# Joined maxima over both halves of the keys in the first unit of an attention kernel, with a second set of key differences

## The chip, the cores and the metric

The kernel runs on one core of one Trainium2 chip, as one launch. The metric is the device time of the launch in microseconds (us), lower being better. A core has five engines that work side by side and wait for each other on semaphores: TensorE (matrix products, shown as PE, its weight loads as PEld), VectorE (DVE), ScalarE (ACT), GpSimd (POOL) and SyncE (SP), which here only issues transfers. Transfers between the chip's main memory and the core's own memory (SBUF) run on 16 DMA engines. Products of TensorE land in PSUM, eight banks of 128 x 512 numbers of 4 bytes, from which VectorE and ScalarE read them.

## The reference

Two independent computations whose results stand side by side in the output. The first (A) is a long convolution over 2048 positions and 448 channels, whose filter is a sum of 256 complex exponentials per channel. The second (B) is full attention with 16 heads of 28 channels:

```python
def _B_ref(x, wqkv, wo):
    B, S, D = x.shape                      # 1, 2048, 448
    H = 16; Dh = D // H
    qkv = (x @ wqkv).reshape(B, S, 3, H, Dh).transpose(2, 0, 3, 1, 4)
    q, k, v = qkv[0], qkv[1], qkv[2]
    scores = jnp.einsum("bhqd,bhkd->bhqk", q, k) * Dh ** -0.5
    p = _softmax(scores, axis=-1)
    o = jnp.einsum("bhqk,bhkd->bhqd", p, v)
    return o.transpose(0, 2, 1, 3).reshape(B, S, D) @ wo
```

All data are 32-bit floats. The softmax needs the largest score of each query before it takes exponentials; the change is about how these maxima are found for one part of the queries.

## The kernel before

**Stages.** The first 204 us hold the *projections* (x times wqkv, as products of split numbers, a high and a low part) and, woven between them, the *seeds* of the convolution's exponentials, computed in eight groups (`seeds(o)`, o = 0 to 7) on ScalarE, VectorE and GpSimd. Then come the maxima of the first unit, and then the *attention loop*, which also carries the rest of the convolution. A *unit* is one group of four heads (`g`, 0 to 3) with one chunk of 512 queries (`c`, 0 to 3); there are 16, and the first is group 0 with chunk 0.

**Projections.** `work` lists the jobs: for each chunk c of 512 positions, `qk_proj(c, s, g)` for four groups and for k (s = 1) and q (s = 0), and four `v_proj`. Each job is twelve matmuls into one of three PSUM tiles (`pm`) and an `evac` that splits the result into a high and a low part on ScalarE and VectorE (tile `hl`, two buffers) and stores it in main memory (`k_d`, `q_d`, `v_d`). For k of chunks 0 and 1 the evacuation also forms *key differences*: the first half of the chunk's keys minus the second half, again as high and low part (`kb`, `dhl`), stored in `kd_d`. The steps `t` of the seeds' pipeline (41 of them) set the pace; projections are spread over the first 37 (`PW`). `ahead` puts loads between the steps: from step `A0` on the first differences, from step `A1` on the first unit's queries. At step 37 the last projection has been issued, the memory of the projection weights (`wst`) is given back, and the pool of the first keys (`k0_p`) takes its place. Up to here a scheduler orders each engine's instructions; from the attention loop on they stand in the order in which the code issues them.

**Maxima.** For a block of 128 queries of one head (16 blocks, index `i`, four heads `j` times four blocks `t`) and 2048 keys, the scores of a block come in four products of 512 columns (`kc` = 0 to 3), each in its own PSUM bank. Because max(a, b) = b + relu(a - b), the first two products are joined: `kc` = 0 multiplies the queries with the key differences (tile `kdif`), and ScalarE takes the Relu into SBUF (tile `rl`, two buffers); `kc` = 1 multiplies them with the second halves of the same two chunks, and one VectorE instruction adds the two and takes the maximum (the custom operation `rl<-pm,rl`). So one pass over 512 columns covers 1024 keys. `kc` = 2 and 3 are plain products with a plain maximum each (`mx<-pm`). `max_join` takes the largest of the three numbers of a block, `max_end` turns them, and `max_put` writes them as two more rows into the query tile. For the first unit the PSUM tiles are taken in turn from a ring of five (`more`: two of `pt`, three of `pm`); in the attention loop the maxima of the next unit run between the other work, with three blocks of lead (`LEAD`).

**Loads.** Keys (`khat`, four tiles of one head each), queries (`qhat`, three buffers, used by the seeds too), differences (`kdif`, one tile a head) and v come back from main memory in rows of 32 partitions, four transfers for a tile. Heads 0 and 1 of the first keys are issued by ScalarE, all other transfers by Sync. Each engine issues in its own order, and a transfer waits for the one eight places before it in the program, so that at most eight are under way. The lines that order the stage:

```python
            if t + 1 == PW:
                project()
                wst.close()
                k0_p = pool(k0_st, "k0_p", side="right")
                for j in range(HG):
                    load_k(0, j, k0_p, nc.scalar if j < 2 else nc.sync)
                load_q(1)
                for c in range(NQ):
                    load_v(0, c)
```

All calls pass through one recording helper, so the profile shows nearly every instruction at line 75 (L75); what is meant is read from the tiles' names.

Of the kernel before, what the change touches and what calls it, by code (L numbers as in the profile page):

```python
# [40 lines left out]
PS = 1  # L41
SGB, XB, XL = 2, 5, 4
K0, KP, KD, UP = 0, 3.5, 5, 3
A0, A1 = 26, 34

N1 = 32
N2 = 64
# [43 lines left out]
def body(ctx, tc, a, out):  # L91
# [11 lines left out]
    dram = ctx.enter_context(tc.tile_pool(name="dram", bufs=1, space=DRAM))  # L103
    k_d = [dram.tile([2, 128, L], F32, name=f"k_{g}") for g in range(G)]
    kd_d = [dram.tile([2, 128, CQ], F32, name=f"kd_{g}") for g in range(G)]
    q_d = [[dram.tile([2, 128, CQ], F32, name=f"q_{g}_{c}") for c in range(NQ)] for g in range(G)]
    sd_d = [dram.tile([BO, 128, SDF], F32, name=f"sd_{o}") for o in range(NO)]
    yu_d = dram.tile([128, N1, D], F32, name="yu_d")
# [46 lines left out]
    def load_kd(g, j, rows=range(4)):  # L155
        if 0 in rows:
            kd_g[g, j] = kd_p.tile([128, CQ], F32R, name=f"kdif{j}")
        t = kd_g[g, j]
        for r in rows:
            nc.sync.dma_start(t[32 * r:32 * r + 32].bitcast(F32), kd_d[g][r % 2, 32 * j:32 * j + 32, :])  # L160

    def load_q(u, rows=range(4)):
        g, c = divmod(u, NQ)
# [3 lines left out]
        for r in rows:  # L167
            nc.sync.dma_start(t[32 * r:32 * r + 32].bitcast(F32), q_d[g][c][r // 2].rearrange("(j p) q -> p j q", j=HG))

    def max_mm(u, i, kc, ps=w_tile):  # L170

        if i == 0 and kc == 0:
            m_u[u] = q_p.tile([128, HG, 4, 3], F32, name="mx", bufs=2)
        j, t = divmod(i, 4)
        pm = ps()
        q, kt = q_u[u][:, j, t * 128:(t + 1) * 128], kt_g[u // NQ][j]
        mx = m_u[u][:, j, t, max(kc - 1, 0):max(kc - 1, 0) + 1]
        if kc == 0:
            nc.tensor.matmul(pm, q, kd_g[u // NQ, j], start=True, stop=True)
            rl_u[u, i] = kd_p.tile([128, CQ], F32, name="rl", bufs=2)  # L180
            nc.scalar.activation(rl_u[u, i], pm, AF.Relu)
        elif kc == 1:
            kb = kt.rearrange("p (c s n) -> p c s n", c=NQ, s=2)[:, :2, 1, :]
            nc.tensor.matmul(pm.rearrange("p (c n) -> p c n", c=2), q, kb, start=True, stop=True)
            rl = rl_u.pop((u, i))
            nc.vector.tensor_tensor_reduce(rl, pm, rl, 1.0, -3.0e38, ALU.add, ALU.max, mx)
        else:
            nc.tensor.matmul(pm, q, kt[:, kc * CQ:(kc + 1) * CQ], start=True, stop=True)
            nc.vector.tensor_reduce(mx, pm, axis=AX.X, op=ALU.max)

    def max_join(u):
        m_u[u, 1] = q_p.tile([128, HG * 4], F32, name="m1", bufs=2)
        nc.vector.tensor_reduce(m_u[u, 1], m_u[u].rearrange("p a b c -> p (a b) c"), axis=AX.X, op=ALU.max)

    def max_end(u, ps):
        nc.tensor.transpose(ps[:16, :128], m_u[u, 1], ident)
# [12 lines left out]
    with ExitStack() as st:  # L209
# [237 lines left out]
        def qk_proj(c, s, g):  # L447
# [9 lines left out]
            def evac():  # L457
                hl = x_p.tile([128, 2, CQ], F32R, name="hl", bufs=2)
                th, tl = hl[:, 0], hl[:, 1]
                if s == 1:  # L460
                    nc.scalar.activation(th, pp, AF.Identity, bias=kones)
                    nc.vector.scalar_tensor_tensor(tl, pp, kones, th.bitcast(F32), op0=ALU.add, op1=ALU.subtract)
                else:
                    nc.scalar.activation(th, pp, AF.Copy)
                    nc.vector.tensor_tensor(tl, pp, th.bitcast(F32), ALU.subtract)
                if s == 1 and c < 2:
                    HC = CQ // 2
                    kb = y_p.tile([128, HC], F32, name="kb")
                    dhl = y_p.tile([128, 2, HC], F32R, name="dhl")
                    dh, dl = dhl[:, 0], dhl[:, 1]  # L470
                    nc.scalar.activation(kb, pp[:, HC:], AF.Copy)
                    nc.vector.tensor_tensor(kb, pp[:, :HC], kb, ALU.subtract)
                    nc.scalar.activation(dh, kb, AF.Copy)
                    nc.gpsimd.tensor_tensor(dl, kb, dh.bitcast(F32), ALU.subtract)
                    nc.sync.dma_start(kd_d[g][:, :, c * HC:(c + 1) * HC].rearrange("i p l -> p i l"), dhl.bitcast(F32))
                nc.sync.dma_start((k_d[g][:, :, c * CQ:(c + 1) * CQ] if s == 1 else q_d[g][c]).rearrange("i p l -> p i l"),
                                  hl.bitcast(F32))
            return evac
# [48 lines left out]
        for t in range(n_stage):  # L527
# [583 lines left out]
```

## Time and profile before

| | |
|---|---|
| time, median of 3 runs | 1360.99 us (1358.85 to 1361.72) |
| the profiled execution | 1363.72 us, its span 1361.9 us |
| busy: PE, DVE, ACT, POOL | 91%, 73%, 71%, 62% of the span |
| granted TensorE clock, mean | 0.976 of full speed |
| moved by DMA | 205.36 MB, 151 GB/s on average |
| chain that ended last | PE 61%, DVE 17%, ACT 12%, the rest 10% |

The profile is one execution on the chip. Its span runs from the first to the last instruction; the rest of the execution's time lies around it. A row of the timeline has a start and a duration in us, the engine, the operation, the tiles written and read (buffer numbers left out), and in brackets the idle time before it with what released it. The chain of work that ended last is followed back from the last instruction. The table of stretches gives each engine's busy time between two moments. Transfers appear as rows of the queue that issued them (SPq, ACTq), which say when they were issued, not when they landed.

### The profile page before, as it was taken

The numbers are of one execution on the slowest core, as the hardware profiler recorded it, in microseconds if no ns is written. First come the engines' busy times: TensorE is split into PE (matmuls) and PEld (weight loads), VectorE is DVE, ScalarE is ACT, GpSimd is POOL, SyncE is SP. The second block draws the span as 40 slices with busy tenths as digits, with TensorE's granted clock in tenths as the row PEclk, the third lists the DMA queues.
The fourth block names the chain that finished last, engine by engine and source line by source line (L and its number), as shares of the span: only waits on it lengthen the run. The fifth ranks groups of instructions, "written<-read, shape, count | busy, mean of one in ns | idle before, by whom it ended". The sixth has DMA issues, their size and how long they took to land.

```text
span 1361.9 us, 33142 instructions
## 1 busy us (share of the span) xinstructions
PE 1243.9 (91%) x12625; PEld 709.8 (52%) x12625; DVE 991.3 (73%) x2138; ACT 966.1 (71%) x2067; POOL 839.5 (62%) x705
## 2 busy tenths in 40 slices
PE   6878885799999999999999999999998999998997
PEld 5657762455555555555555555555555545544433
DVE  5897886877777777777788888888887766857311
ACT  4876752488888888888888887878786655655553
POOL 3685681278877878878888988888895111202221
PEclk9988987899999999999999999999999999999999
DMA  6677669636675545378534233632325534636476
GB/s 197 199 261 266 225 212 271 179 74 150 147 164 118 128 135 159 111 202 198 162 94 97 56 73 86 146 79 67 79 65 140 189 116 161 206 111 203 138 192 176
DMA packets 200089, 205.36 MB, mean 151 GB/s; under 512 B 95993, under 2 KB 158521, under 8 KB 197881
## 3 DMA queue, kind: packets, MB, share of 16 engines
q1 hardware_dynamic: 199544, 201.13, 53.2%
q10 hardware_dynamic: 384, 2.10, 0.6%
q8 instruction: 100, 1.64, 0.5%
q14 instruction: 61, 0.49, 0.1%
HBM read 120.73 MB, written 82.18 MB: 149 GB/s over the span
## 4 chain that ended last, share of the span: by engine, by line
PE 61%; DVE 17%; ACT 12%; issue 3%; DMA 3%; POOL 3%; SPq 0%; ACTq 0%; DVEq 0%; POOLq 0%
PE pm L75 35%; PE po L75 13%; PE pss L75 12%; ACT p L75 6%; DVE mx L75 4%; DVE g L75 2%; DVE tri L75 2%; ACT rl L75 2%; DVE p L75 2%; POOL qhat L75 1%; DVE pr L75 1%; DVE zg L75 1%; DVE rl L75 1%; DVE sg L75 1%; ACT tri L75 1%
## 5 line engine op out<-in xcount | busy, mean ns | idle before, releaser
L75 ACT ACTIVATE p<-pss 128x512 f32<-128x512 f32 x1024 | 565.4, 609 | 138.5 <-PE pss L75 127.5
L75 PE MATMUL pss<-qhat,khat 128*128 128x512 f32 x1024 | 403.1, 400 | 3.3 <-ACT p L75 3.3
L75 DVE TENSOR_REDUCE mx<-pm 128x1 f32<-128x512 f32 x500 | 321.4, 683 | 116.3 <-PE pm L75 115.1
L75 PE MATMUL pm<-khat,qhat 128*128 128x512 f32 x749 | 330.1, 444 | 41.4 <-DVE mx L75 36.5
L75 POOL TENSOR_TENSOR e<-e,sdb 128x256 f32<-128x256 f32 x168 | 201.8, 1201 | 171.9 <-ACT e L75 162.9
L75 PE MATMUL po<-p,v 128*32 128x512 f32 x2048 | 271.9, 599 | 0.0
L75 POOL TENSOR_TENSOR e<-e,eu 128x256 f32<-128x256 f32 x168 | 248.1, 1477 | 13.2
L75 PEld LDWEIGHTS pm<-khat,qhat 128*128 128x128 f32 x749 | 142.0, 190 | 216.0 <-DVE mx L75 79.8
L75 PEld LDWEIGHTS pss<-qhat,khat 128*128 128x128 f32 x1024 | 191.1, 189 | 46.7 <-ACT p L75 11.2
L75 DVE CUSTOM_DVE_ANT_0 rl<-pm,rl 128x512 f32<-128x512 f32 x249 | 171.4, 688 | 48.3 <-ACT rl L75 43.8
L75 POOL TENSOR_TENSOR eu<-e,sdb 128x256 f32<-128x256 f32 x168 | 201.7, 1201 | 0.0
L75 DVE TENSOR_TENSOR g<-g,zg 128x128 f32<-128x128 f32 x392 | 162.9, 416 | 46.3 <-ACT zg L75 41.3
L75 ACT ACTIVATE rl<-pm 128x512 f32<-128x512 f32 x249 | 151.2, 607 | 20.7 <-PE pm L75 18.8
L75 POOL TENSOR_TENSOR p<-pr,pr 64x448 f32<-64x448 f32 x32 | 40.9, 1277 | 191.6 <-DVE pr L75 180.5
L75 PE MATMUL pm<-kdif,qhat 128*128 128x512 f32 x249 | 101.6, 408 | 2.2 <-DVE mx L75 1.5
L75 PEld LDWEIGHTS pm<-e,g 128*32 128x32 f32 x3584 | 63.0, 110 | 52.8 <-issue 30.8
L75 DVE TENSOR_TENSOR zg<-g,zg 128x128 f32<-128x128 f32 x224 | 87.5, 391 | 1.9
L75 PEld LDWEIGHTS po<-p,v 128*32 128x32 f32 x2048 | 56.6, 110 | 42.7 <-issue 38.0
L75 PE MATMUL pm<-xh,wh 112*128 112x512 f32 x128 | 56.8, 448 | 22.3 <-DVE hl L75 10.8
L75 PE MATMUL pm<-e,g 128*32 128x64 f32 x3584 | 72.5, 220 | 0.0
L75 ACT ACTIVATE y<-pm 128x448 f32<-128x448 f32 x48 | 26.3, 548 | 63.0 <-PE pm L75 30.7
L75 DVE TENSOR_TENSOR pr<-pm,ub 128x448 f32<-128x448 f32 x64 | 37.0, 619 | 32.7 <-PE pm L75 32.7
(137 smaller groups left out, 1571.8 us busy)
## 6 DMA issues: line engine op xcount, KB each, us to landing
sdb<-sd SPq DMA_DIRECT2D x56, 336.0 KB
qhat<-q SPq DMA_DIRECT2D x64, 256.0 KB
khat<-k SPq DMA_DIRECT2D x56, 256.0 KB
sd<-sg SPq DMA_DIRECT2D x8, 1456.0 KB
k<-hl SPq DMA_DIRECT2D x16, 512.0 KB
q<-hl SPq DMA_DIRECT2D x16, 512.0 KB
mw<-in_mw SPq DMA_DIRECT2D x16, 512.0 KB
sd<-qhat SPq DMA_DIRECT2D x8, 896.0 KB
```

The lines of the kernel that those rows point to most:

```text
L75: i = f(*args, **kw)
```

## The change

- The evacuation forms key differences for chunks 2 and 3 too, for group 0 alone, and stores them in a new place, `kd_d[4]`.
- For the first unit, `kc` = 2 and 3 become a second joined pair: differences of chunks 2 and 3 (new tile `kd2`), Relu, joined maximum. Its Relu tiles come from a new pool `k2_p` with three buffers, and `max_join` takes two numbers a block instead of three. All other units keep one pair and two plain maxima.
- The four tiles of differences become one tile `kdif` with four parts. For group 0 it is loaded in four transfers (one of the 32-partition rows for all heads, from step 27) instead of sixteen (from step 26). Later groups load it head by head as before.
- The first unit's queries are issued from step 25 instead of 34.
- The second differences are loaded by Sync in four transfers, between the issue of head 1's keys and that of head 2's, into memory that the projection weights held.
- The second unit's queries and v of group 0 are issued after the last steps of the seeds instead of right after the keys.

```diff
-A0, A1 = 26, 34
+A0, A1 = 27, 25
...
+    kd_d.append(dram.tile([2, 128, CQ], F32, name="kd2"))
...
+    kd_t = kd_p.tile([128, HG, CQ], F32R, name="kdif")
+
+    def load_kd(g, j):
+        kd_g[g, j] = kd_t[:, j, :]
+        for r in range(4):
+            nc.sync.dma_start(kd_t[32 * r:32 * r + 32, j, :].bitcast(F32), kd_d[g][r % 2, 32 * j:32 * j + 32, :])
+
+    def load_kd_row(r, g=0, t=kd_t):
+
+        kd_g.update({(g, j): t[:, j, :] for j in range(HG)})
+        nc.sync.dma_start(t[32 * r:32 * r + 32].bitcast(F32), kd_d[g][r % 2].rearrange("(j p) q -> p j q", j=HG))
...
-    def max_mm(u, i, kc, ps=w_tile):
+    def max_mm(u, i, kc, ps=w_tile, p2=None):
...
-        mx = m_u[u][:, j, t, max(kc - 1, 0):max(kc - 1, 0) + 1]
-        if kc == 0:
-            nc.tensor.matmul(pm, q, kd_g[u // NQ, j], start=True, stop=True)
-            rl_u[u, i] = kd_p.tile([128, CQ], F32, name="rl", bufs=2)
+        n = kc // 2 if p2 else max(kc - 1, 0)
+        mx = m_u[u][:, j, t, n:n + 1]
+        if kc == 0 or kc == 2 and p2:
+            nc.tensor.matmul(pm, q, kd_g[G if kc else u // NQ, j], start=True, stop=True)
+            rl_u[u, i] = (p2 or kd_p).tile([128, CQ], F32, name="rl", bufs=3 if p2 else 2)
             nc.scalar.activation(rl_u[u, i], pm, AF.Relu)
-        elif kc == 1:
-            kb = kt.rearrange("p (c s n) -> p c s n", c=NQ, s=2)[:, :2, 1, :]
+        elif kc == 1 or kc == 3 and p2:
+            kb = kt.rearrange("p (c s n) -> p c s n", c=NQ, s=2)[:, kc - 1:kc + 1, 1, :]
...
-    def max_join(u):
+    def max_join(u, n=3):
...
-                if s == 1 and c < 2:
+                if s == 1 and (c < 2 or g == 0):
...
-                    nc.sync.dma_start(kd_d[g][:, :, c * HC:(c + 1) * HC].rearrange("i p l -> p i l"), dhl.bitcast(F32))
+                    nc.sync.dma_start(kd_d[g if c < 2 else G][:, :, c % 2 * HC:(c % 2 + 1) * HC].rearrange("i p l -> p i l"), dhl.bitcast(F32))
...
-        for i in range(2 * HG):
-            ahead[A0 + i].append(lambda i=i: load_kd(0, i // 2, range(2 * (i % 2), 2 * (i % 2) + 2)))
+        for i in range(4):
+            ahead[A0 + i].append(lambda i=i: load_kd_row(i))
...
+                k2_p = pool(st, "k2_p", side="right")
                 for j in range(HG):
+                    if j == 2:
+                        k2_t = k2_p.tile([128, HG, CQ], F32R, name="kd2")
+                        for r in range(4):
+                            load_kd_row(r, G, k2_t)
                     load_k(0, j, k0_p, nc.scalar if j < 2 else nc.sync)
-                load_q(1)
-                for c in range(NQ):
-                    load_v(0, c)
+        load_q(1)
+        for c in range(NQ):
+            load_v(0, c)
         xst.close()
...
-                max_mm(0, i, kc, more[(4 * i + kc) % 5])
-        max_join(0)
+                max_mm(0, i, kc, more[(4 * i + kc) % 5], k2_p)
+        max_join(0, 2)
```

More of the change, by code (lines that the diff above doesn't have):

```diff
@@ L153, in load_v @@
         nc.sync.dma_start(t.rearrange("p t h e -> p t (h e)"), v_d[c][:, g])
[L155 to L160, printed above, removed]
+    kd_t = kd_p.tile([128, HG, CQ], F32R, name="kdif")
[6 more added lines that the diff above has]
+        nc.sync.dma_start(t[32 * r:32 * r + 32].bitcast(F32), kd_d[g][r % 2].rearrange("(j p) q -> p j q", j=HG))
     def load_q(u, rows=range(4)):
@@ L189, in max_mm @@
             nc.vector.tensor_reduce(mx, pm, axis=AX.X, op=ALU.max)
-    def max_join(u):
+    def max_join(u, n=3):
         m_u[u, 1] = q_p.tile([128, HG * 4], F32, name="m1", bufs=2)
-        nc.vector.tensor_reduce(m_u[u, 1], m_u[u].rearrange("p a b c -> p (a b) c"), axis=AX.X, op=ALU.max)
+        nc.vector.tensor_reduce(m_u[u, 1], m_u[u].rearrange("p a b c -> p (a b) c")[:, :, :n], axis=AX.X, op=ALU.max)
     def max_end(u, ps):
```

## Prediction

> **What bounds the kernel now.** I read the table of stretches first, because the change touches one stage only, then the chain of work that ended last, then the timeline inside that stage, and last the queue of Sync. In the table the columns are the stretch, its length, busy time (and instructions) of TensorE's matmuls, its weight loads, VectorE, ScalarE and GpSimd, then the granted clock, the DMA engines' share and their rate in GB/s.
>
> ```profile
> 80.00:120.00 40.00, 30.02 (x105) 24.19 (x106) 32.86 (x58) 29.70 (x62) 29.14 (x34) 0.79 0.67 223
> ...
> 204.30:217.85 13.55, 0.01 (x2) 0.03 (x1) 3.19 (x6) 2.22 (x6) 3.47 (x4) 0.64 1.04 285
> 217.85:222.00 4.15, 3.96 (x8) 2.21 (x9) 2.21 (x4) 1.21 (x3) 0.00 (x0) 0.53 1.04 310
> 222.00:241.40 19.40, 16.03 (x42) 6.90 (x42) 19.07 (x44) 6.50 (x11) 0.00 (x0) 1.00 1.05 259
> 241.40:251.00 9.60, 6.07 (x15) 3.70 (x15) 8.21 (x19) 1.86 (x4) 0.00 (x0) 0.82 0.75 268
> ```
>
> From 204.3 to 217.85 every engine is nearly empty and the DMA engines are full. From 222 to 241.4 VectorE is busy 19.07 of 19.40 us, and the DMA engines are full again. So two resources hold the first unit: transfers up to 217.85, VectorE behind it. The chain says what the first wait is made of:
>
> ```profile
> 196.12 7.99 PE pm L75 x24
> 204.11 6.44 DMA khat<-k
> 210.93 6.78 DMA qhat<-q
> 217.85 1.19 PE pt L75 x2
> ```
>
> The last projection ends at 204.1. Then a row of the first keys flies for 6.44 us, and only when it has landed does Sync issue the last two rows of the first queries, which fly 6.78 us. In the program each transfer waits for the one eight places ahead of it, so at most eight are under way; that is why one flight follows another.
>
> Inside the stage, from the timeline (start, duration, engine, operation; in brackets the idle time before it and its releaser):
>
> ```profile
> 225.74 0.68 DVE L75 CUSTOM_DVE_ANT_0 rl<-pm,rl 128x512 f32<-128x512 f32 x1
> ...
> 226.58 0.47 PE L75 MATMUL pm<-khat,qhat 128*128 128x512 f32 x1 [0.20 <-DVE mx L75]
> ...
> 227.07 0.50 PE L75 MATMUL pt<-kdif,qhat 128*128 128x512 f32 x1
> 227.40 0.40 PE L75 MATMUL pm<-khat,qhat 128*128 128x512 f32 x1
> 227.55 0.68 DVE L75 CUSTOM_DVE_ANT_0 rl<-pm,rl 128x512 f32<-128x512 f32 x1
> 227.60 0.60 ACT L75 ACTIVATE rl<-pt 128x512 f32<-128x512 f32 x1 [0.58 <-PE pt L75]
> ...
> 228.25 0.73 PE L75 MATMUL pt<-khat,qhat 128*128 128x512 f32 x2 [0.45 <-ACT rl L75]
> ```
>
> One block of 128 queries costs VectorE one joined maximum (custom) and two plain ones: 227.55 - 225.74 = 1.81 us, 0.60 each, sixteen times. The other rows give the handoffs that I need below: joined maximum to the matmul that reuses its buffer 0.84 (225.74 to 226.58); matmul to the next matmul 0.33 (227.07 to 227.40); difference matmul to its Relu 0.53 (227.07 to 227.60); Relu to the matmul that reuses its buffer 0.65 (227.60 to 228.25). The stage's one stall and its end:
>
> ```profile
> 242.14 0.73 PE L75 MATMUL pm<-kdif,qhat 128*128 128x512 f32 x1 [1.31 <-DVE mx L75]
> 242.66 0.63 PE L75 MATMUL pm<-khat,qhat 128*128 128x512 f32 x1
> 242.90 0.60 ACT L75 ACTIVATE rl<-pm 128x512 f32<-128x512 f32 x1 [1.44 <-PE pm L75]
> ...
> 243.44 0.69 DVE L75 CUSTOM_DVE_ANT_0 rl<-pm,rl 128x512 f32<-128x512 f32 x1 [1.35 <-PE pm L75]
> ...
> 250.79 0.20 DVE L75 TENSOR_REDUCE m<-mx 128x16 f32<-128x48 f32 x1
> ...
> 251.26 0.47 PE L75 MATMUL pm<-kdif,qhat 128*128 128x512 f32 x1
> ```
>
> The maxima are joined at 250.79; the second unit's lead begins at 251.26. The attention loop behind has the same order and waits on every engine in both programs, so what this stage gains or loses moves the end by the same amount.
>
> **The change part by part.** *Projections.* Two more difference evacuations (group 0, chunks 2 and 3). What eight of them cost now (a row of waits: in total, times, longest):
>
> ```profile
> PE pm L75 <- DVE kb L75: 6.4, 4, 3.4
> ```
>
> That is 0.8 us each, 1.6 for two. Against it Sync issues four loads of the first differences where it issued sixteen, and the first queries leave the busy last stretch. The scheduler also lays the projections out anew (ScalarE's last sines now stand ahead of the last six projections). I take +1.0 for the end of the projections (205.3); bounds -2 and +3.4 (the longest such wait).
>
> *Start of the pairs.* First queries and first differences now land during the projections. What is late next is the second set of differences: its first row waits for the last projection, since its memory is that of the projection weights. In Sync's queue behind it stand the stores of the last k and q, then its other three rows, and the last of them waits for the third row of head 0's keys. ScalarE issues that row after two evacuations, as here:
>
> ```profile
> 207.12 9.75 ACTq L75 DMA_DIRECT2D khat<-k  x5
> ```
>
> In the chain's terms: 3.0 (204.1 to 207.1) + 6.44 + 6.78 = 16.2, taken as 16 us after the last projection, where the queries took 13.55. ScalarE is free of its issues at 216.87 now, 12.8 after the projections, and should be so again. From below 12: less is in flight when the queries are gone, so some 4.5 a flight, an estimate two thirds of the two above. From above by bytes: 1.05 MB of differences, 1.05 of head 0's keys, half of head 1's, 1.05 of stores, 0.9 of seeds and about 1.0 (estimate) still in flight make 5.5 MB, at 285 GB/s 19.4 us.
>
> *The pairs.* Per block two joined maxima replace one and two plain ones: at 1.81 / 3 = 0.603 each VectorE alone would need 1.21 and not 1.81. But ScalarE's Relus double, and five score buffers go round in turn, two for a pair: the key matmul of a pair takes the buffer that the Relu of two pairs before left, the difference matmul that of the joined maximum of three pairs before, and the program puts the key matmul first. Relu to key matmul 0.65, to difference matmul 0.33, to Relu 0.53: 1.51 for two pairs; in each fifth pair the difference goes first, 1.18. Mean (4 x 1.51 + 1.18) / 10 = 0.72 a pair. The other ring is shorter: (0.84 + 0.53 + 0.60) / 3 = 0.66. So 0.72, bounds 0.603 (VectorE back to back) and the slow clock's value: by 242.14 to 242.90, 0.65 + 0.52 + 0.76 = 1.93 and 1.41, mean 0.91.
>
> From the landing of the second differences: first pair 0.76 + 0.60 = 1.36; thirty more at 0.72 = 21.6; the last joined maximum 0.69. TensorE comes out of an empty stretch, so the 4.15 us at clock 0.53 hold 4.6 pairs that are 0.19 longer: 0.9. At head 3 three difference matmuls stand ahead of the first key matmul and the last waits for head 2's last maximum: 0.84 + 0.33 + 0.50 for 0.72, +0.95, of which two quick maxima win back 0.2: 0.7. After such a gap (1.31 us of TensorE) the clock fell to 0.82 for the stretch; half of 3 us at the slow pace, 0.3. Together 25.6.
>
> On the clock the Trainium skill ("TensorE: Matmul & The Clock Gate", section "Part 1: The HAM clock gate (the "warmup" mystery)") says that the array starts slow, is released after some 3.4 us of steady work and falls back only after an idle window as long. The start here agrees (4.15 us at 0.53, then 1.00); the stall at 242 does not, since a gap of 1.31 us was enough. By the page the 0.3 would be zero.
>
> *Next queries and v.* They move behind head 2's and 3's keys and the last seeds' stores. Sizes in KB:
>
> ```profile
> qhat<-q SPq DMA_DIRECT2D x64, 256.0 KB
> khat<-k SPq DMA_DIRECT2D x56, 256.0 KB
> sd<-sg SPq DMA_DIRECT2D x8, 1456.0 KB
> k<-hl SPq DMA_DIRECT2D x16, 512.0 KB
> ...
> sd<-qhat SPq DMA_DIRECT2D x8, 896.0 KB
> ```
>
> and where they stood:
>
> ```profile
> 226.97 3.82 SPq L75 DMA_DIRECT2D qhat<-q  x4
> ...
> 237.74 0.37 SPq L75 DMA_DIRECT2D sd<-qhat  x1
> ```
>
> The store at 237.74 waits for row 1 of those queries, so they were in by about 240 and never waited for. Afterwards, from the last projection: keys 4.2 MB, differences 1.05, stores 1.05, seeds 0.9 + 2.4, queries 1.05, in flight 1.0: 11.6 MB. The three full stretches moved 13.55 x 285 + 4.15 x 310 + 19.40 x 259 = 10.2 MB in 37.1 us, 274 GB/s: 42 us. By flights (eight at a time) I come to about 37. Mean 40: 205.3 + 40 = 245.3, hidden under the maxima; from 42 it begins to show. v follows 4 us later and is not needed for some 10.
>
> *Nothing.* One tile for four differences (later loads go head by head with the waits they had), three Relu buffers, a join over two columns: no wait changes.
>
> **Sum.** 205.3 + 16 + 25.6 = 246.9 against 250.8: 3.9 us less. On the profiled run's own time, 1363.7, that is 1359.8; it stands 2.7 above the median of the three runs, 1361.0, from which I forecast 1357.1.
>
> **The rivals.** *A, as summed*: 1357.1, own range 1353.5 to 1360.5 (start 16 -3/+3).
>
> *B, VectorE's pace*: the pairs run at 0.603 and the differences land after 13.5, with no delay of the projections: 204.3 + 13.5 + 1.36 + 18.1 + 0.69 + 1.9 = 239.9; then the next queries decide, 204.3 + 37 = 241.3, 9.5 less: 1351.5. For it: 19.07 of 19.40 busy shows VectorE can be fed; against it: that was with one Relu in three, and the ring above.
>
> *C, the clock stays down*: the pairs leave TensorE a short hole each time, and the gap at 242 shows that short holes suffice. At 0.91 the 21.6 become 27.3, less the 1.2 for slow spells already counted: 30.1, end 251.4, 0.6 later than now: 1361.6. Against it: 222 to 241.4 ran at 1.00 with holes in every block. The Trainium skill has this as a rule on the same page, section "A second HAM failure mode: psum-queue depth-cycling": frequent short idling between groups of matmuls makes the clock swing. The 222 row speaks against that here, the 241.4 row for it.
>
> *D, slower: the next queries come late.* One mechanism: the second unit's lead waits for queries that now stand behind 3.4 MB more (second differences, last seeds). It decides the end when 11.6 MB need more than 46 us, below 252 GB/s, and makes the kernel measurably slower below 238. At the 223 of the stretch 80 to 120 they need 52 us: 257.3, 6 later than 251.26: 1367. Against it: all four full stretches are above 252; for it: more small stores among them.
>
> *E, the change does not do what it says*: the new layout of the projections loses what the pairs win (+3.4 at the projections, differences at 19.4 after them): 207.7 + 19.4 + 25.6 = 252.7: 1362.9.
>
> **How the numbers follow.** Chances: A 0.50, B 0.15, C 0.15, D 0.13, E 0.07. No change means within 0.2%, 2.7 us, about what a measurement of this kernel can tell. Faster: 0.37 of A (its upper end lies within) and all of B, 0.52. Same: 0.13 of A, 0.07 of C, 0.04 of E, 0.24. Slower: 0.08 of C, D, 0.03 of E, 0.24. The range leaves out half of B and nearly all of D: 1351.5 to 1364.
>
> **What would show it.** Right: the first matmul of the stage waits for the second differences at about 221; joined maxima 0.72 apart with VectorE idle a little before each, released by ScalarE or TensorE; no plain maxima in the stage; the join near 247. Wrong in a step: differences landing before 217 or after 224; joined maxima 0.60 apart (B) or 0.9 with a clock near 0.5 (C); the second unit's first matmul waiting for a transfer (D); the last projection ending outside 202 to 208 (E).

## The result and the profile after

The changed kernel took 1369.77 us (median of 11 runs, 1366.66 to 1372.04) against 1361.77 us (median of 11, 1358.85 to 1366.49) for the kernel before on the same chip: ratio 1.005, 95% interval 1.0036 to 1.0064. It is 0.5% slower, where 3.9 us less was forecast. The profiled execution took 1370.22 us, its span is 1368.4 us, 6.5 more than before.

The table of stretches of the changed kernel, with the columns of the prediction's:

```profile
180.00:204.00 24.00, 17.78 (x63) 13.51 (x62) 14.64 (x30) 12.72 (x29) 11.15 (x17) 0.78 0.53 185
204.00:215.54 11.54, 9.21 (x24) 6.64 (x24) 7.44 (x16) 1.87 (x4) 9.13 (x14) 0.70 0.95 342
215.54:222.00 6.46, 0.79 (x1) 0.29 (x1) 1.35 (x2) 1.18 (x2) 0.00 (x0) 0.70 1.04 261
222.00:232.00 10.00, 1.19 (x2) 0.50 (x2) 0.70 (x2) 0.99 (x3) 0.00 (x0) 0.50 1.06 282
232.00:242.00 10.00, 7.93 (x20) 4.49 (x20) 5.79 (x17) 5.64 (x10) 0.00 (x0) 0.67 1.03 231
242.00:251.00 9.00, 8.53 (x26) 4.08 (x25) 8.74 (x28) 7.47 (x15) 0.00 (x0) 1.00 1.04 338
251.00:258.60 7.60, 5.10 (x17) 2.54 (x17) 6.16 (x21) 4.73 (x9) 0.00 (x0) 1.00 0.90 211
```

TensorE still projects after 204, for 11.2 us more (the last matmul ends at 215.5; before, at 204.3). GpSimd, which had 3.47 us of seeds left behind 204.3, has 9.13 left: the seeds are late too. Then come 18 us in which the DMA engines are full and the others nearly empty, and then the pairs. The chain that ended last, in order of time, names the links:

```profile
195.61 9.81 DMA sd<-qhat
...
205.47 1.59 POOL qhat L75 x5
...
208.18 0.80 DVE qhat L75 x2
...
210.11 0.75 DVE hl L75
...
210.91 4.62 PE pm L75 x12
...
216.98 6.59 DMA khat<-k
223.59 9.67 DMA kd<-kd
...
233.39 0.78 PE pm L75
```

A store of seeds flies 9.81 us; the last group's seeds are built in the tile that it leaves; VectorE multiplies them and only then evacuates a projection (`hl`) for which TensorE stands still; the last projection follows; then a flight of keys and a flight of second differences. In the chain of before no store of seeds holds the last projections: the last 24 matmuls run without a break from 196.12.

The pairs and their end, from the timeline:

```profile
240.05 0.69 DVE L75 CUSTOM_DVE_ANT_0 rl<-pt,rl 128x512 f32<-128x512 f32 x1
...
240.85 0.69 DVE L75 CUSTOM_DVE_ANT_0 rl<-pm,rl 128x512 f32<-128x512 f32 x1
...
241.47 0.69 DVE L75 CUSTOM_DVE_ANT_0 rl<-pm,rl 128x512 f32<-128x512 f32 x1
...
257.28 0.69 DVE L75 CUSTOM_DVE_ANT_0 rl<-pm,rl 128x512 f32<-128x512 f32 x1
...
258.02 0.19 DVE L75 TENSOR_REDUCE m<-mx 128x16 f32<-128x32 f32 x1
...
258.59 0.47 PE L75 MATMUL pm<-kdif,qhat 128*128 128x512 f32 x1
```

Joined maxima only, and the second unit's lead at 258.59 without a wait for its queries. From landing to join the stage takes 24.6 us (233.4 to 258.0), where one difference for a block took 32.9. So 8.3 us are won in the pairs, 4.4 lost before them in the longer landing (17.9 against 13.5) and 11.2 in the projections: 7.2 net at the join (250.8 to 258.0), 6.5 of it in the span. In this pair of profiles the whole loss is there by the join.

### The profile page after: what moved, and what is told of

It is laid out like the page before. It is cut to its first block, busy times and chain, and to the rows that moved or that the text cites. A ratio compares the mean times of both kernels' runs of the same rounds, so it can differ in the third digit from the quotient of the medians.

```text
span 1368.4 us, 33169 instructions
## 1 busy us (share of the span) xinstructions
PE 1244.0 (91%) x12625; PEld 710.0 (52%) x12625; DVE 982.3 (72%) x2140; ACT 978.0 (71%) x2087; POOL 835.8 (61%) x707
## 3 DMA queue, kind: packets, MB, share of 16 engines
q8 instruction: 100, 1.64, 0.5%
## 4 chain that ended last, share of the span: by engine, by line
PE 61%; DVE 15%; ACT 12%; DMA 4%; issue 3%; POOL 3%; SPq 1%; ACTq 0%; POOLq 0%; DVEq 0%
PE pm L75 36%; PE po L75 13%; PE pss L75 12%; ACT p L75 6%; DVE mx L75 3%; DVE g L75 2%; ACT rl L75 2%; DVE p L75 2%; POOL qhat L75 2%; DVE tri L75 1%; DVE pr L75 1%; DMA sd<-qhat 1%; DVE px L75 1%; DVE zg L75 1%; DVE qhat L75 1%
## 5 line engine op out<-in xcount | busy, mean ns | idle before, releaser
L75 DVE TENSOR_REDUCE mx<-pm 128x1 f32<-128x512 f32 x480 | 308.4, 684 | 104.5 <-PE pm L75 103.3
L75 PE MATMUL pm<-khat,qhat 128*128 128x512 f32 x739 | 326.8, 444 | 41.1 <-DVE mx L75 36.0
L75 PE MATMUL po<-p,v 128*32 128x512 f32 x2048 | 271.9, 598 | 0.0
L75 DVE CUSTOM_DVE_ANT_0 rl<-pm,rl 128x512 f32<-128x512 f32 x259 | 178.4, 690 | 51.9 <-ACT rl L75 48.8
L75 ACT ACTIVATE rl<-pm 128x512 f32<-128x512 f32 x259 | 156.4, 605 | 13.1 <-PE pm L75 12.2
L75 PEld LDWEIGHTS po<-p,v 128*32 128x32 f32 x2048 | 56.6, 110 | 42.6 <-issue 38.0
L75 ACT ACTIVATE y<-pm 128x448 f32<-128x448 f32 x48 | 26.3, 548 | 63.2 <-PE pm L75 30.8
```

Of the source, the lines that this page charges most:

```text
L75: i = f(*args, **kw)
```

## The experiments

One row for each run. "Last projection" is where its last matmul ends, "first pair" the first matmul with second differences (in kernels without pairs: the matmul whose wait for a transfer opens the maxima), "join" the reduction of the first unit's maxima, all in us of the profiled execution; the ratio is to the kernel before on the same chip.

| run | last projection | first pair | join | ratio, 95% interval |
|---|---|---|---|---|
| before | 204.3 | 217.9 | 250.8 | 1 |
| changed | 215.5 | 233.4 | 258.0 | 1.0050 (1.0036 to 1.0064) |
| e1 | 203.9 | 230.2 | 255.0 | 1.0028 (1.0012 to 1.0044) |
| e2, no pairs | 213.8 | 224.0 | 259.1 | 1.0055 (1.0032 to 1.0078) |
| e3, no pairs | 204.3 | 217.3 | 250.8 | 0.9986 (0.9969 to 1.0002) |
| e4, no pairs | 203.4 | 216.8 | 250.3 | 1.0009 (0.9986 to 1.0032) |
| e5 | 216.9 | 236.3 | 260.6 | 1.0062 (1.0043 to 1.0081) |
| e6 | 217.4 | 230.7 | 256.8 | 1.0061 (1.0041 to 1.0080) |
| e7, no pairs | 203.8 | 218.9 | 250.9 | 1.0001 (0.9983 to 1.0018) |
| e8 | 210.5 | 227.6 | 252.6 | 1.0024 (1.0009 to 1.0038) |
| e9 | 208.7 | 232.1 | 256.2 | 1.0050 (1.0031 to 1.0069) |
| e10 | 212.9 | 245.8 | 271.9 | 1.0163 (1.0139 to 1.0188) |
| e11 | 208.3 | 226.4 | 250.5 | 0.9994 (0.9977 to 1.0011) |
| e12 | 206.1 | 224.3 | 248.7 | 0.9985 (0.9969 to 1.0000) |
| e13 | 206.4 | 227.6 | 252.0 | 1.0009 (0.9993 to 1.0025) |
| e14 | 209.0 | 229.9 | 254.4 | 1.0028 (1.0014 to 1.0042) |
| e15 | 209.2 | 217.8 | 251.3 | 1.0009 (0.9994 to 1.0025) |
| e16 | 209.9 | 222.3 | 248.6 | 0.9996 (0.9977 to 1.0016) |
| e17, no pairs | 203.1 | 216.6 | 250.6 | 1.0026 (1.0010 to 1.0043) |
| e18 | 214.7 | 231.9 | 256.1 | 1.0044 (1.0025 to 1.0064) |

Time follows the join: a straight line through the table (ratios times 1362 us) gives an estimate of 0.9 to 1.0 us for each us, near the prediction's one for one. e17 lies farthest from it (below).

**Which part of the change costs the projections (e1, e2, e3, e4, e7).** e1 is the changed kernel with the first queries back at step 34 (`A0, A1 = 27, 34`), e2 the kernel before with them at step 25:

```diff
-A0, A1 = 26, 34
+A0, A1 = 26, 25
```

> The changed kernel with one number back: the first unit's queries issued from step 34, as before the change, everything else as changed. Theory P (the early queries hold one of three buffers that the seeds use too, the last seeds wait 9.4 us for a store, and this delays the projections): GpSimd has no wait on that store, the last projection ends near 207 instead of 215.5, the maxima join near 251 to 254, time within 0.3% of the kernel before (about 1361 to 1366). Rival R (the two added evacuations and the new layout of the projections did it, the queries are innocent): last projection still at 213 or later, time 1368 or more.

> The kernel before with the first unit's queries issued from step 25 instead of 34 and nothing else. Theory P: GpSimd waits for a store of the seeds again (5 us or more), the last projection ends at 209 or later, and since the first matmul of the maxima then waits for head 0's keys only (about 11 after the last projection), the join is at 209 + 11 + 32.5 = 252.5 or later: time 1363 or more. Rival R: last projection at 204, join at 248, time about 1358.

e1's projections end at 203.9, e2's at 213.8: the early queries alone make the loss, with or without pairs. e1 stays slower all the same, since its second differences now fly behind the queries and land 26.3 us behind the projections.

e3 is the kernel before, which also computes and stores group 0's differences of chunks 2 and 3 (nothing reads them); e4 has the next queries and v loaded behind the branch, as the change does; e7 has the four loads and the one tile of the first differences:

```diff
-                if s == 1 and c < 2:
+                if s == 1 and (c < 2 or g == 0):
...
-                load_q(1)
-                for c in range(NQ):
-                    load_v(0, c)
+        load_q(1)
+        for c in range(NQ):
+            load_v(0, c)
...
-        for i in range(2 * HG):
-            ahead[A0 + i].append(lambda i=i: load_kd(0, i // 2, range(2 * (i % 2), 2 * (i % 2) + 2)))
+        for i in range(4):
+            ahead[A0 + i].append(lambda i=i: load_kd_row(i))
```

> The kernel before with the key differences of chunks 2 and 3 of group 0 formed and stored as well, but never loaded. Theory P: 0 to 2 us on the end of the projections, time 1361 to 1364. Rival R: the last projection ends 5 us later or more, time 1367 or more.

> The kernel before with the second unit's queries and v issued after the last steps of the seeds. Both theories: the queries land near 246, before they are needed at 251, no change (1360 to 1363). If they land late (rival D of the prediction): the second unit's first matmul waits for a transfer and the time grows by 2 us or more.

> The kernel before, in which only the first differences come in four loads of four heads each (from step 27 on) in place of sixteen from step 26 on. All else is as before: one difference for a block, the first queries from step 34 on. All theories: Sync has twelve issues fewer in the last projections, none of which stood on the path; last projection 203 to 206, join 249 to 252, ratio within 0.998 to 1.002. Outside of it the four loads would be a cause of their own.

All three are level with the kernel before. The two evacuations, priced at 1.6 us, cost nothing that the profile shows.

**Tiles or order (e5, e8, e9).** In the changed kernel a seed memset on GpSimd waited for a store:

```profile
205.47 0.51 POOL L75 MEMSET qhat<- 128x112 f32 x2 [9.37 <-DMA sd<-qhat]
```

The queries take one of the three `qhat` tiles nine steps sooner, which leaves two for groups 5 to 7. My first theory was that this is the cause. e5 takes it away: group 5 is built in the memory of the v tiles, empty until then.

```diff
+                if o == 5:
+                    se = v_t.rearrange("p n t h e -> p (n t h e)")
+                else:
```

> The changed kernel with one thing different: the sixth group of seeds (o = 5) is built in the memory of the v tiles, which is empty until the first unit, so that the early first queries take no buffer from the seeds: every group again follows the group three before it. Theory P (the loss is the seeds' buffer alone): no memset of a seed tile waits more than 1.5 us for a store, the last projection ends at 204 to 206 and not at 215.5, the second differences land 16 to 18 us later, the pairs take the 24.6 us that they took, so the join comes at 245 to 248 and the kernel is 3 to 6 us faster than before (ratio 0.9955 to 0.998). Rival R (the early transfers of queries and differences themselves, or the new order of the projections, hold the projections): the last projection still ends after 210, the join after 252, ratio 1.001 or more.

No memset waits, and the projections end at 216.9: the theory fell. What VectorE does in e1 (first fence) and in the changed kernel (second), from the timelines:

```profile
173.97 0.74 DVE L75 SCALAR_TENSOR_TENSOR hl<-pm,kones,hl 128x512 fp32r<-128x512 f32 x1
...
177.60 0.67 DVE L75 TENSOR_TENSOR hl<-pm,hl 128x512 fp32r<-128x512 f32 x1
178.20 0.25 DVE L75 TENSOR_SCALAR tri<-pn 128x112 f32<-128x112 f32 x1
...
185.33 1.95 DVE L75 TENSOR_TENSOR tri<-tri 128x1232 f32<-128x1232 f32 x1
```

```profile
175.06 0.28 DVE L75 TENSOR_SCALAR tri<-pn 128x112 f32<-128x112 f32 x1 [3.63 <-ACT tr L75]
...
179.71 1.44 DVE L75 TENSOR_TENSOR tri<-tri 128x1232 f32<-128x1232 f32 x1
181.07 0.74 DVE L75 SCALAR_TENSOR_TENSOR hl<-pm,kones,hl 128x512 fp32r<-128x512 f32 x1
...
191.05 0.68 DVE L75 TENSOR_TENSOR hl<-pm,hl 128x512 fp32r<-128x512 f32 x1
...
198.08 0.75 DVE L75 SCALAR_TENSOR_TENSOR hl<-pm,kones,hl 128x512 fp32r<-128x512 f32 x1 [3.94 <-ACT hl L75]
```

In e1 two evacuations of chunk 3 precede the six phase instructions (`tri`) of the last seed group; in the changed kernel the six stand first, the first evacuation comes 7.1 us later and the second 13.5, because more products of the seeds stand between them too. In these timelines VectorE takes its instructions in the order in which the scheduler laid them. The Trainium skill says the same ("PSUM — Partial Sum Buffer", section "Engine vs sequencer instructions"): the queues of ScalarE, VectorE and GpSimd are strict FIFO.

Seeds and evacuations then hold each other up. Sync issues in its own order too, and group 5's seeds stand behind two stores of v that wait for ScalarE's evacuations of v. In e1 (first fence) they leave at 181.57, in the changed kernel (second) 14.0 us later, and group 7 waits for their tile:

```profile
167.95 9.91 SPq L75 DMA_DIRECT2D v<-vst  x2
...
181.57 1.28 SPq L75 DMA_DIRECT2D sd<-qhat  x1
```

```profile
184.44 7.34 SPq L75 DMA_DIRECT2D v<-vst  x2
...
195.61 1.28 SPq L75 DMA_DIRECT2D sd<-qhat  x1
```

In e5, where that tile is free, VectorE waits for the other tile of the same group, which goes two in turn in every version (the changed kernel has this wait too, 2.27 us at 201.11):

```profile
204.45 0.93 DVE L75 TENSOR_TENSOR sg<-tri 128x336 f32<-128x336 f32 x2 [2.28 <-DMA sd<-sg]
```

e8 and e9 are the changed kernel with the queries at steps 28 and 32 (`A1 = 28`, `A1 = 32`).

> The changed kernel with the first queries loaded from step 28 on, not 25: they are taken from the pool behind the sixth group's seed tile and stand in Sync's queue behind the last group's inputs, and the order of instructions on VectorE and ScalarE is nearly that of the run with the queries at step 34; but the seventh and eighth groups still have two seed tiles in turn, as in the changed kernel. Theory O (the loss is the order: with the queries' loads ahead of the last group's inputs in Sync's queue the last group's phases are laid ahead of the first evacuation of chunk 3 and every later evacuation is late): the last projection ends at 203 to 207, the queries have landed by then, the second differences come 16 to 18 us later, the pairs take 24.6, the join is at 245 to 249; ratio 0.9955 to 0.9985. Theory B (the loss is the seeds' tiles in turn, in spite of the run with the sixth group in v's memory): a seed memset waits 5 us or more for a store, the last projection ends after 209, ratio 1.001 or more.

> The changed kernel with the first queries from step 32 on: their tile is taken behind the seventh group's, so that all seeds keep the tiles that they had in the kernel before; in Sync's queue the queries stand some eight transfers ahead of where the run with step 34 had them. Both theories: the last projection ends at 204 to 208 (its last two evacuations stand behind a little more of the last seeds on VectorE). The queries land before 212, so that the second differences are what the pairs wait for, 16 to 20 us after the projections; join 246 to 251; ratio 0.996 to 1.000. If the queries' position costs nothing here and the ratio is still above 1.001, then the pairs with second differences loaded behind the projections do not pay at all, wherever the queries stand.

e8 came out as theory B had it, with VectorE's order nearly that of e1: the two evacuations of chunk 3 stand ahead of the phases again, yet one memset waits 7.80 us and the projections end at 210.5. Sync and GpSimd in e8:

```profile
189.17 1.27 SPq L75 DMA_DIRECT2D sd<-qhat  x1
...
199.66 0.56 POOL L75 MEMSET qhat<- 128x112 f32 x2 [7.80 <-DMA sd<-qhat]
```

What differs is on ScalarE: one evacuation of v is laid later (at 184.32; in e1 at 176.78), and Sync sits 17.93 us in the two stores of v where e1 sat 9.91, with group 5's seeds behind them. So the order on ScalarE, with Sync's queue behind it, can cost what I put down to VectorE. In the changed kernel both orders are new.

e9 missed its forecast by both theories: the last evacuations wait behind group 7's products (208.7), and its second differences land 23.4 us later.

**Another queue for the queries (e11 to e14).** The four query loads are issued by ScalarE (e11, e12) or GpSimd (e13, e14) at the same step 25; e12 and e14 also have group 5 in v's memory.

```diff
-            ahead[A1 + i].append(lambda i=i: load_q(0, range(2 * i, 2 * i + 2)))
+            ahead[A1 + i].append(lambda i=i: load_q(0, range(2 * i, 2 * i + 2), nc.scalar))
```

> The changed kernel with the four loads of the first queries issued by ScalarE, not Sync, at the same step 25. The seeds' tiles stay two in turn, and the scheduler lays the last evacuations differently: VectorE has the four last pairs of hl spread among the seeds, none of the last group's phases ahead of the first one. Theory O (laid order): last projection 203 to 207, queries in long before, second differences 16 to 18 us later, join 245 to 249, ratio 0.9955 to 0.999. Theory B (tiles in turn): a seed memset waits 4 us or more for a store, last projection 208 to 212, join 250 to 255, ratio 0.999 to 1.004.

> The kernel of the run with the queries on ScalarE's queue, and the sixth group's seeds in the memory of v: the order of instructions on TensorE, VectorE and ScalarE is the same to the instruction, only the tiles differ, so that this pair of runs prices the tiles alone. Theory B: last projection 203 to 206, 4 us or more ahead of its twin; join 245 to 248; ratio 0.9955 to 0.998. Theory O: last projection and join within 1.5 us of its twin. If both runs end the projections after 208, neither is the whole and the early transfers themselves are to be looked at.

> The changed kernel with the four loads of the first queries issued by GpSimd at step 25. Sync's queue then has the last group's inputs where the run with the queries at step 34 has them, and the order on VectorE and ScalarE is nearly that run's; the seeds' tiles are two in turn. Theory O: last projection 203 to 207, join 245 to 249, ratio 0.9955 to 0.999. Theory B: a seed memset waits 5 us or more, last projection 208 to 212 as with the queries at step 28, ratio 1.000 to 1.004.

> As the run with the queries on GpSimd's queue, with the sixth group's seeds in v's memory: tiles free, and of the order only the last four evacuations laid later on VectorE, behind the last group's first products. Theory B: last projection 203 to 206, ratio 0.9955 to 0.998. Theory O: 205 to 210, by what stands ahead of the last four evacuations, without any memset that waits; ratio 0.997 to 1.002.

e13 keeps the tiles two in turn and the step, and wins back 9.1 of the 11.2 us (206.4). On VectorE, from its timeline, the evacuations stand where e1 has them:

```profile
176.51 0.74 DVE L75 SCALAR_TENSOR_TENSOR hl<-pm,kones,hl 128x512 fp32r<-128x512 f32 x1
180.04 0.68 DVE L75 TENSOR_TENSOR hl<-pm,hl 128x512 fp32r<-128x512 f32 x1
180.64 0.26 DVE L75 TENSOR_SCALAR tri<-pn 128x112 f32<-128x112 f32 x1
```

e11 and e12 have the same order of instructions on TensorE, VectorE and ScalarE. e12's projections end 2.1 us sooner, but the two profiles stand 1.6 us apart already in chunk 1, long before a tile could matter. From TensorE's timeline in e11 and in e12:

```profile
83.48 0.79 PE L75 MATMUL pm<-xh,wh 112*128 112x512 f32 x1 [5.28 <-DVE hl L75]
```

```profile
81.88 0.79 PE L75 MATMUL pm<-xh,wh 112*128 112x512 f32 x1 [5.34 <-DVE hl L75]
```

So in this pair of profiles the shared tiles cost 0.5 us. One order spans more than that: at the matmul above the profiles lie between 80.9 and 83.5, and e15 and e16 (below), with e12's order on these three engines and its tiles, end their projections 3.1 and 3.8 us later. Last projections less than 4 us apart therefore say little, such as e14's, which freed the tiles and was 2.6 us later than e13 (209.0), the way its order would have it. None of the four reached a ratio that theory O had set for it; e11's and e13's fall in theory B's range, but without the memset wait of 4 us or more that B needs (0.71 us in e11, none in e13). e12 is the fastest version seen, 0.15% below the kernel before, with an interval that just reaches 1. But e3, which only adds work to the kernel before, stands at 0.14% below, so no version is shown to beat it.

**Inputs or order (e18).** With the queries on Sync's queue the last group's inputs stand behind them. e18 moves only these inputs ahead.

```diff
-                slots[max(SP * o + (i or -2), 0)] += st_
+                slots[max(SP * o + (i or (-4 if o == 7 else -2)), 0)] += st_
```

> The changed kernel with one number changed: the last group's inputs (four loads of nat, o = 7) are loaded two steps sooner, so that they stand ahead of the first queries in Sync's queue; the queries stay on Sync's queue at step 25, the tiles stay two in turn, and the scheduler still lays the last group's six phase instructions ahead of the first evacuation of chunk 3 on VectorE. Theory O (what counts is the order on VectorE): nothing is won, the first such evacuation again comes behind the phases, the last projection ends at 213 to 218, ratio 1.003 to 1.007. Rival I (what counts is that the inputs come late, behind the queries): the inputs are in some 8 us sooner, the last projection ends at 204 to 208, join 246 to 251, ratio 0.996 to 1.000.

VectorE and GpSimd in e18:

```profile
176.98 1.44 DVE L75 TENSOR_TENSOR tri<-tri 128x1232 f32<-128x1232 f32 x1
178.34 0.75 DVE L75 SCALAR_TENSOR_TENSOR hl<-pm,kones,hl 128x512 fp32r<-128x512 f32 x1
188.75 0.69 DVE L75 TENSOR_TENSOR hl<-pm,hl 128x512 fp32r<-128x512 f32 x1 [1.26 <-ACT hl L75]
```

```profile
203.80 0.51 POOL L75 MEMSET qhat<- 128x112 f32 x2 [10.49 <-DMA sd<-qhat]
```

The inputs are issued from 144.0 instead of 155.6. The phases are 2.7 us sooner and still ahead of the first evacuation, the second again 10 us behind it, and the projections end at 214.7. So the late inputs are not the cause.

**The landing of the second differences (e6, e10, e15, e16).** e6 is e5 with the second differences loaded from step 34 on into the memory of the input rows. e10 is e8 with them in v's memory, and v loaded behind the last pair. e15 and e16 are e12 with sixteen loads of one head's row and eight of two heads', each ahead of its keys:

```diff
...
+                    for r in range(4):
+                        nc.sync.dma_start(k2_t[32 * r:32 * r + 32, j, :].bitcast(F32), kd_d[G][r % 2, 32 * j:32 * j + 32, :])
                     load_k(0, j, k0_p, nc.scalar if j < 2 else nc.sync)
```

> The kernel of the run with the seeds in v's memory, and besides the second differences are loaded during the last projections: their tile takes the memory of the input rows x, which are dead once chunk 3 is transposed (x then has one tile for a chunk where it had three halves in turn). After the projections only keys, stores and the next queries are left to move. Theory L (the 16 to 18 us of landing are flights of the second differences behind one another): the first pair starts when head 0's keys are in, 7 to 11 us after the last projection, the pairs then go at 0.7 us or at the pace at which the heads' keys arrive, and the join is at 236 to 244, 4 to 10 us sooner than with the seeds alone; the second unit then waits for its queries until 241 to 246; ratio 0.990 to 0.996. Rival M (the stage is bound by the bytes moved behind the projections, keys above all): the pairs start early but stall head by head, the join is within 2 us of the run with the seeds alone (245 to 248), and the ratio is the same as there.

> As the run with the queries at step 28, and the second differences are loaded from step 34 on into the memory of the v tiles, which are loaded behind the last pair instead. Theories O and L (the landing of the second differences is flights behind one another, not bytes): last projection 203 to 207, the first pair when head 0's keys are in, 7 to 11 us later, the pairs then held by the keys of each head; join 236 to 244, the second unit's queries in by 243 to 247; the first weighted sums, 13 us behind the join, find v in; ratio 0.991 to 0.997. Rival V (v then comes late): the first sums wait for v by 2 to 6 us, ratio 0.996 to 1.001. Theory B: last projection after 209, ratio 0.998 to 1.003.

> The kernel of the run with the queries on ScalarE's queue and the sixth seeds in v's memory, with the second differences loaded head by head (sixteen loads of 64 KB, each head's four ahead of its keys) where they came in four loads of 256 KB. Theory L (the landing is a flight behind a flight, and the first pair needs one head alone): last projection 205 to 207, the first pair starts 9 to 14 us later and not 18, the pairs are then held by the keys of each head; join 243 to 247, the second unit's queries in by 245 to 248; ratio 0.996 to 0.998. Rival M (bytes, and sixteen issues at 0.4 to 1.2 us in Sync's queue ahead of the keys of heads 2 and 3): the join stays at 248 to 251, ratio 0.998 to 1.001.

> The same with eight loads of 128 KB, two heads each. Theory L: between its neighbours, first pair 12 to 16 us behind the last projection, join 245 to 248, ratio 0.9965 to 0.9985. Rival M: join 248 to 250, ratio 0.998 to 1.0005.

The smaller loads do start the pairs sooner, 8.6 us (e15) and 12.4 us (e16) behind the last projection instead of 18.2 (e12), but the join is no earlier (251.3 and 248.6 against 248.7). TensorE in e15, from the timeline:

```profile
224.28 0.79 PE L75 MATMUL pt<-khat,qhat 128*128 128x512 f32 x1 [4.11 <-ACT rl L75]
...
231.41 0.47 PE L75 MATMUL pm<-khat,qhat 128*128 128x512 f32 x1 [1.81 <-DMA khat<-k]
```

The longer stall is for a Relu, not for keys. ScalarE stood in its own issues of keys, and its next instruction waited 10.46 us for a flight of keys in e15 and 10.10 in e16; the first Relus start at 223.6 and 223.8. In e16 no matmul of the pairs waits for keys. From the last projection to the join e12 took 42.6 us, e15 42.0, e16 38.7, so e16's loads won 3.9 us in the stage, about as much as its projections ended later. e6 won 3.7 us at the join over e5, between what theories L and M allow. Smaller flights set the first matmul (theory L); that bytes set the join (theory M) is not shown.

e6 shows rival D's wait: its second unit's first matmul stands 2.34 us for the next queries at 259.75, behind a join at 256.8. e10 failed for a reason that I had not written down. ScalarE and TensorE in e10, from the timeline:

```profile
219.82 24.19 ACTq L75 DMA_DIRECT2D khat<-k  x7
```

```profile
245.09 0.80 PE L75 MATMUL pt<-khat,qhat 128*128 128x512 f32 x1 [13.75 <-ACT rl L75]
```

Eight loads of 128 KB joined the last stores, a seeds' store took 15.54 us, and ScalarE, which issues heads 0 and 1 of the keys, sat 24 us in those issues with the Relus of the first pairs behind them.

**Do the pairs pay (e17).** e17 is the kernel before with the queries issued by ScalarE at step 25 and group 5 in v's memory: e12 without pairs.

> The kernel before, with one difference for a block as it was, and only the first queries moved: from step 25, issued by ScalarE, and the sixth group's seeds in v's memory. This is the change's early queries without its pairs and without the second differences. If the pairs are what pays (theory A): the first block starts when head 0's keys are in, 7 to 11 us behind a last projection at 204 to 208, VectorE takes the 32.9 us that it took, join 246 to 250, ratio 0.997 to 1.000, no better than its twin with pairs. If the second differences cost what the pairs win (theory N): the stage starts 7 to 10 us sooner than with them and is 8 us longer, join 243 to 247, ratio 0.9955 to 0.998, better than the twin's 0.9985.

Theory A by the profile: without second differences the first maximum comes no sooner than before (216.6, 13.5 us behind the projections), because now it waits for head 0's keys,

```profile
216.55 0.76 PE L75 MATMUL pt<-khat,qhat 128*128 128x512 f32 x1 [9.54 <-DMA khat<-k]
```

and the join stays at 250.6. With pairs, e12 joins 1.9 us sooner in spite of projections that end 3.1 later. By the runs, too, e12 is the better twin, though on another chip (0.9985 against 1.0026, intervals apart). But e17's median, 1366.55 us, lies well above its own profiled run (1362.06), so that profile doesn't show what made the others slower; this stays open.

## Why the prediction was wrong

**The step that failed is "Projections": +1.0, bounds -2 and +3.4; it measured +11.2.** Its items were sized one by one, and of these the evacuations (e3) and the four loads (e7) came out at nothing. The item named last, "the scheduler also lays the projections out anew", was the one that counted, and I gave it the longest wait for an evacuation in the old order as a bound. A wait in one order bounds nothing in another. The order of the changed kernel could be read before the run: six phase instructions of the last seeds ahead of the first evacuation of chunk 3 on VectorE. I noted the like of it for ScalarE only, and gave it no price of its own. I also took "the first queries leave the busy last stretch" as a gain; it is what brought the new order, as e1 and e2 show from both sides. Shown: the early queries on Sync's queue cost 9.5 us (e2 against before) to 11.6 (the changed kernel against e1), freeing the shared tiles does not win it back (e5), nor do earlier inputs (e18), and the same queries at the same step from another queue cost 2 to 5 (e11 to e14), and nothing without pairs (e17). Inferred from the timelines: that the new order does it, on VectorE, or on ScalarE with Sync's stores behind it. No run changed one engine's order and nothing else, so which of them counts stays open.

**"Start of the pairs"** was mis-sized: 16 against 17.9, inside its bounds. The chain was right, a flight of keys and a flight of differences, but the second took 9.67 us and not 6.78, while the flight of keys began 1.4 us behind the last projection and not 3.0. In the eight versions that load them in four rows behind early queries (the changed kernel, e5, e8, e11 to e14, e18) the landing took 17.1 to 21.3.

**"The pairs"** came out in size: 24.6 against 25.6 us, and 0.72 us a pair over all 31 steps (234.83 to 257.28). The limit that the prediction named, the ring over ScalarE's Relus, did not hold at full clock. There the pace was 0.69 (16 steps from 240.05 to 251.07) with VectorE busy 8.74 of 9.00 us, between the ring's 0.72 and rival B's 0.60; the mean comes to 0.72 through the slow first pairs and one step of 1.64 us at head 3, so its exactness is in part luck. Rival C's clock did not come: granted 1.00 from 242 to the end. The Trainium skill's rule on short holes between groups of matmuls ("TensorE: Matmul & The Clock Gate", section "A second HAM failure mode: psum-queue depth-cycling") does not show in these pairs.

**"Next queries and v"** and **"Nothing"** held: the lead did not wait, and e4 and e7 are level.

**The sum.** With the measured terms and the old end of the projections, 204.3 + 17.9 + 24.6 = 246.8, which is the forecast's 246.9 by luck: 1.9 more in the landing against 1.0 less in the pairs and the 1.0 that the forecast had put on the projections, small errors beside the large one. **Rival E** had the right mechanism, a new layout that loses what the pairs win, at 0.07 and with 3.4 us for it; it should have had a price of its own, and more chance.

## What to carry to other kernels

Where a scheduler lays the instructions, a transfer that is moved on a queue can reorder every engine: compare the order of every engine that empties the matmul's buffers, instruction by instruction, and of the queue that stores what they write; price each evacuation by what now stands ahead of it, not by the waits of the old order. A load issued early is free only if what it is issued ahead of, and whose buffer it takes, is not late then. Starting a stage sooner with smaller loads gains little when another engine of the stage is still held then, as ScalarE was in its issues of keys.

## What the runs showed of the hardware

- **The time of a run goes with its granted clock.** Over 35 runs of the kernel before beside e11 to e14, those at a mean clock of 0.980 took 1358.0 to 1358.5 us, those at 0.966 to 0.967 took 1365.9 to 1367.1. That is 0.6 us for each 0.001, and a spread as large as the change's effect; one profiled run says little about a median. Whether the clock makes the time or the two have a common cause, no run shows.
- **Flights lengthen to 10 us and more.** Rows of 256 KB took 3.4 to 10.7 us between the last projection and the join (3.44 and 10.71 on the chains of e15 and e14), while the changed kernel moved 231 to 338 GB/s in all. Taking the queries off Sync's queue did not shorten them: e12's differences landed 18.2 us behind the projections, the changed kernel's 17.9. The Trainium skill ("DMA: Bandwidth & Descriptors", section "Issuing engines are not separate DMA queues") says that transfers run on the same DMA engines whoever issues them, and that a second issuer saves issue time only. The 9.1 us that another issuer saved in e13 came with another order of the evacuations (above), which that rule does not cover.
- **An engine that issues transfers can be held by them**: 24.19 us on ScalarE in e10, with the Relus queued behind.
